# A decode step of attention plus a gated feed-forward layer: fewer and larger weight loads, and a new order of the last K and V

## The chip, the cores and the metric

The kernel runs on one core of a Trainium2 chip. The metric is the device time of one execution in microseconds (us). A profile gives a span some 2 us shorter than the device time of the same execution (523.8 us for 525.59 in the kernel before).

## The reference, cut to what matters

Four tokens (one for each of 4 sequences) are normalised, and the sum of three things is returned: x itself, sliding-window attention, and a gated feed-forward layer.

```python
xn = layernorm(x)                                    # (4, 1, 640)
q  = xn @ wq                                         # 32 heads of 192
s  = softmax(q . K[:, :, 6144:8192] / sqrt(192))     # the last 2048 of 8192 keys
y1 = (s . V[:, :, 6144:8192]).reshape(4, 1, 6144) @ wo                # wo (6144, 640)
y2 = (silu(xn @ w1) * (xn @ w3)) @ w2                # w1, w3 (640, 1536), w2 (1536, 640)
return x + y1 + y2
```

K and V of one head over the window and all four sequences are 3,072 KB each; 64 such loads are nearly all of the 223 MB that the kernel reads, and there is little arithmetic for each byte.

## The kernel before

All large loads are issued, in the order of the program, by one queue (the sync engine's, SPq in the profile). x's small load is issued by the scalar engine. The program is a table of slots, four for each head, and the sync engine waits for a buffer to be free before it issues the load into it. The parts that matter here:

```python
    def load_k(h):                                   # two K buffers
        kt = kpool.tile([P, NJ, Dh], BF16, tag="kt")
        nc.sync.dma_start(out=..., in_=k_win[:, h]...)
    def load_v(h, n=1):                              # three V buffers
        vt = vpool.tile([P, NJ, Dh], BF16, tag="vt")
    ...
    x_sb = const.tile([B, D], BF16, name="x_sb")
    nc.scalar.dma_start(out=x_sb[:], in_=A_x.rearrange("b s d -> (b s) d"))
    for k0 in range(0, KC, 2):                       # KC = 5: wq in three transfers, in V's buffers
        n = min(2, KC - k0)
        wt = vpool.tile([P, 2, H * Dh], BF16, tag="vt")
        nc.sync.dma_start(out=wt[:, 0:n, :]..., in_=wq_v[:, k0:k0 + n, :]...)
    for h in range(KBUFS):
        load_k(h)                                    # K0, K1
    # ... layer norm of x (vector and scalar engine), transposes of it (PE)
    # q = xn @ wq: two passes over six PSUM banks, 60 matmuls of 128x512, into qbc
    # ... clears of three PSUM tiles (vector engine)
    def mult(u):                                     # u = 4 h + g: quarter g of head h
        nc.vector.tensor_tensor(out=pr[:], in0=kts[h][:, g*JQ:(g+1)*JQ, :], in1=qbc[...], op=ALU.mult)
    ...
    for h in range(H):
        u0, ul = h * GQ, h * GQ + GQ - 1
        if h >= KBUFS:
            add((h - KBUFS + 1) * GQ, 0, load_k, h)  # K2 in slot 4: when K0's four products are done
        if h < H - 2:
            add(u0 + 2, 0, load_v, h)
        for u in range(u0, ul + 1):
            add(u, 1, mult, u)
    ...
    add(3, 0, w1_load)                               # 1.7 MB, between V0 and K2
    for n in range(4):
        add(4 + 2 * n, 1, w1_low, n)                 # w1's remaining rows, 12 partitions wide
    ...
    for h in range(H - 2, H):                        # the end of the queue
        add(NU - 6, 0, load_v, h)
    add(NU - 6, 0, w2_load, 0); add(NU - 6, 0, w2_load, 1)
    add(NU - 6, 0, wo_load, NG - 2); add(NU - 6, 0, wo_load, NG - 1)
    add(NU - 6, 0, w2_load, 2); add(NU - 6, 0, w2_load, 3)
```

So the first loads stand in the queue as wq, K0, K1 (issued at once), then V0 and w1 (when the projection has read wq's first two rows), then K2.

## Time and profile before

| | before |
|---|---|
| median of 3 runs | 525.7 us (525.61 to 526.16) |
| span of the profile | 523.8 us |
| busy: PE, vector engine (DVE), scalar engine (ACT) | 69%, 65%, 11% |
| load queue | 223.26 MB, 11,904 packets, 426 GB/s over the span |

The first view is the page's strip of 40 slices of 13.1 us: tenths in which the 16 load engines were busy, and what they moved.

```profile
DMA  9999999999999999999999999999999999999996
GB/s 389 422 443 425 433 431 432 428 433 432 430 435 428 437 418 446 424 437 426 434 434 429 432 434 429 435 427 435 425 437 434 427 437 431 430 434 425 441 418 275
```

Only the last slice is not full. Stretches of the span show the same (columns: length, busy time and instructions of PE, weight loads, DVE, ACT, POOL, then granted PE clock, share of the load engines' time, GB/s):

```profile
40.00:50.00 10.00, 6.59 (x31) 0.57 (x5) 8.79 (x9) 2.05 (x5) 0.00 (x0) 1.00 1.03 436
50.00:510.00 460.00, 325.19 (x2127) 69.40 (x1521) 311.62 (x358) 45.25 (x156) 0.00 (x0) 0.89 1.00 431
```

The load engines are busy from the first microseconds to the end (a share of 0.85 in the first 5 us, of 1.00 from 50 to 510), and no trace of this case moved more than 432 GB/s from 50 to 510 us. So the time of the kernel is the work in the queue, plus what stands before the first packet, plus what stands behind the last landing. The first part of the timeline of the sync queue, of DVE and of PE (start, length, engine, line, operation, count) shows how the head runs.

```profile
6.68 0.48 DVE L177 CAST xf<-x_sb 4x640 f32<-4x640 bf16 x1 [3.80 <-DMA x_sb<-in_A_x_dram]
```

PE, the projection:

```profile
15.15 14.93 PE L243 MATMUL qps<-wt,xnT 128*128 128x512 bf16 x59
```

And the sync queue, the issues of V0 and of K2:

```profile
26.22 0.54 SPq L132 DMA_DIRECT2D vt<-in_A_v_cache_dram  x1
...
41.62 0.54 SPq L125 DMA_DIRECT2D kt<-in_A_k_cache_dram  x1
```

The projection runs from 15.15 to about 30.1 us. The end, on PE:

```profile
519.21 0.98 PE L264 MATMUL acc<-wo_t,oT 128*4 128x320 bf16 x12 [0.47 <-DMA wo_t<-in_A_wo_dram]
520.38 0.71 PE L264 MATMUL acc<-w,hT 128*4 128x320 bf16 x8 [0.19 <-DMA w<-in_B_w_dram]
```

The same end in the chain of waits (start, length, what):

```profile
489.68 30.66 DMA w<-in_B_w_dram
520.38 0.76 PE acc L264 x8
521.13 0.47 DVE res L542
```

Three things were also read from the records of single packets in the trace, which have a start, a length, a size and a queue. Packets of one size take almost the same time everywhere: 9 ns for 4 B, 55 ns for 1,280 B, 912 ns for 24,576 B (the first ones of wq take 1.3 to 1.9 us, and 19 later ones, beside instruction fetches, 1.2 to 1.5); between the last two sizes that is 27.2 GB/s. The 16 engines do not end together: five end their last packet at 517.2 to 518.6 us, eleven at 519.6 to 520.5. And 15 packets of 16,384 B are instruction fetches and take about 0.94 us of an engine each. A "landing" below is the end of a load's last packet.

### The profile page before, as it was taken

The page shows a single profiled execution, that of the slowest core. Times are in us where ns is not written, and L with a number is a line of the kernel's source. Part 1 is how long each engine was busy: PE and PEld are TensorE (multiplying, and loading weights), DVE is VectorE, ACT ScalarE, POOL GpSimd, SP SyncE. Part 2 cuts the span into 40 slices and gives each one's busy share as a digit, 9 for nine tenths or more (in the row PEclk, how much of TensorE's full clock was granted, in tenths as well). Part 3 has the DMA queues.
Part 4 walks back from the last instruction along what each step waited for, and adds up shares of the span by engine and source line. Part 5 has one row for each costly group of instructions (what it writes and reads, how often), then busy time and mean ns, then how long its engine had stood idle before and what let it go on. Part 6 is the DMA issues. An engine that isn't in the chain of part 4 may idle for free.

```text
span 523.8 us, 4820 instructions
## 1 busy us (share of the span) xinstructions
PE 361.8 (69%) x2336; PEld 75.9 (14%) x1643; DVE 340.9 (65%) x413; ACT 55.8 (11%) x176; POOL 5.6 (1%) x12
## 2 busy tenths in 40 slices
PE   0965866887668776667547768586686876675685
PEld 0100111121111111111111111111111111111122
DVE  3268853687656767577646877466667766667671
ACT  2111111111001110101100111001101110011111
POOL 4000000000000000000000000000000000000000
PEclk9979886898878998789997988889878898889988
DMA  9999999999999999999999999999999999999996
GB/s 389 422 443 425 433 431 432 428 433 432 430 435 428 437 418 446 424 437 426 434 434 429 432 434 429 435 427 435 425 437 434 427 437 431 430 434 425 441 418 275
DMA packets 11904, 223.26 MB, mean 426 GB/s; under 512 B 1332, under 2 KB 1608, under 8 KB 3052
## 3 DMA queue, kind: packets, MB, share of 16 engines
q1 hardware_dynamic: 11868, 222.96, 99.2%
q8 instruction: 15, 0.25, 0.2%
q14 instruction: 5, 0.04, 0.0%
q10 hardware_dynamic: 16, 0.01, 0.0%
HBM read 222.96 MB, written 0.01 MB: 426 GB/s over the span
## 4 chain that ended last, share of the span: by engine, by line
DMA 60%; PE 20%; DVE 15%; ACT 3%; issue 1%; SPq 1%
DMA kt<-in_A_k_cache_dram 44%; PE ps L288 11%; DMA w<-in_B_w_dram 11%; DVE pr L277 10%; DMA vt<-in_A_v_cache_dram 5%; PE po L361 4%; PE qps L243 3%; DVE sc L296 2%; ACT ex L324 1%; DVE z L332 1%; DMA x_sb<-in_A_x_dram 1%; PE mt L318 1%; ACT L324 0%; ACT negm L321 0%; PE mt L305 0%
## 5 line engine op out<-in xcount | busy, mean ns | idle before, releaser
L288 PE MATMUL ps<-pr,idb 128*128 128x512 bf16 x768 | 214.7, 422 | 137.6 <-DVE pr L277 137.5
L277 DVE TENSOR_TENSOR pr<-kt,qbc 128x3072 bf16<-128x3072 bf16 x128 | 223.5, 1746 | 104.0 <-DMA kt<-in_A_k_cache_dram 104.0
L296 DVE TENSOR_REDUCE sc<-ps 128x16 f32<-128x512 f32 x128 | 87.1, 681 | 2.7 <-PE ps L288 2.6
L340 PE MATMUL o_ps<-vt,z 128*8 128x384 bf16 x1024 | 60.5, 380 | 0.2 <-DVE z L332 0.2
L361 PE MATMUL po<-o_sb,sel_w 128*32 128x192 f32 x128 | 49.2, 518 | 0.6 <-ACT o_sb L343 0.6
L340 PEld LDWEIGHTS <-z 128*8 128x8 bf16 x1024 | 26.2, 95 | 98.8 <-issue 89.2
L332 DVE TENSOR_TENSOR z<-ex,mask_b 128x256 bf16<-128x256 bf16 x32 | 13.5, 423 | 38.6 <-ACT ex L324 38.6
L343 ACT COPY o_sb<-o_ps 128x384 f32<-128x384 f32 x32 | 15.3, 478 | 196.9 <-PE o_ps L340 196.9
L313 ACT ACTIVATE gneg<-gmax 1x128 f32<-1x128 f32 x32 | 9.8, 308 | 162.8 <-DVE gmax L310 162.8
L305 PEld LDWEIGHTS mt<-idf,lmax 128*1 128x1 f32 x32 | 3.2, 101 | 127.5 <-issue 125.5
L361 PEld LDWEIGHTS po<-o_sb,sel_w 128*32 128x32 f32 x128 | 13.8, 130 | 29.4 <-issue 27.9
L288 PEld LDWEIGHTS <-idb 128*128 128x128 bf16 x124 | 12.0, 97 | 39.3 <-issue 32.8
L318 PEld LDWEIGHTS mt<-ones_ff,gneg 1*128 1x128 f32 x64 | 9.6, 186 | 47.1 <-issue 43.7
L243 PE MATMUL qps<-wt,xnT 128*128 128x512 bf16 x59 | 14.9, 412 | 0.1
L318 PE MATMUL mt<-ones_ff,gneg 1*128 1x1 f32 x64 | 12.3, 259 | 0.7 <-ACT gneg L313 0.7
L321 ACT COPY negm<-mt 128x1 f32<-128x1 f32 x32 | 5.1, 159 | 70.4 <-PE mt L318 70.4
L310 DVE TENSOR_REDUCE gmax<-mt 1x4 f32<-1x128 f32 x32 | 8.8, 274 | 5.8 <-PE mt L305 5.8
L348 PEld LDWEIGHTS po<-rsum,tot_w 128*32 128x32 f32 x64 | 4.4, 108 | 51.5 <-ACT ex L324 35.4
L249 DVE CAST qbc<-qps 128x512 bf16<-128x512 f32 x6 | 3.8, 684 | 11.7 <-PE qps L243 11.7
L324 ACT ACTIVATE ex<-sc,negm 128x64 bf16<-128x64 f32 x32 | 11.1, 348 | 1.0
L305 PE MATMUL mt<-idf,lmax 128*1 128x128 f32 x32 | 10.9, 340 | 0.0
L199 PE MATMUL xnT_ps<-idb,xn 4*128 4x4 bf16 x5 | 0.4, 178 | 13.4 <-DVE xn L194 13.4
(74 smaller groups left out, 84.4 us busy)
## 6 DMA issues: line engine op xcount, KB each, us to landing
kt<-in_A_k_cache_dram SPq DMA_DIRECT2D x32, 3072.0 KB, 19.1
vt<-in_A_v_cache_dram SPq DMA_DIRECT2D x32, 3072.0 KB, 25.5
wo_t<-in_A_wo_dram SPq DMA_DIRECT2D x8, 960.0 KB, 20.7
wt<-in_A_wq_dram SPq DMA_DIRECT2D x2, 3072.0 KB
w<-in_B_w_dram SPq DMA_DIRECT2D x1, 1920.0 KB
wt<-in_A_wq_dram SPq DMA_DIRECT2D x1, 1536.0 KB, 19.5
w<-in_B_w_dram SPq DMA_DIRECT2D x1, 1536.0 KB
w<-in_B_w_dram SPq DMA_DIRECT2D x2, 640.0 KB
```

Source lines behind the costliest of these rows:

```text
L243: nc.tensor.matmul(qp[:], lhsT=xnT[:, kc].rearrange("p a b -> p (a b)"), rhs=wq_rows[kc][:, (c0 + i) * QC:(c0 + i + 1) * QC], start=(kc == ...
L277: nc.vector.tensor_tensor(out=pr[:], in0=kts[h][:, g * JQ:(g + 1) * JQ, :], in1=qbc[:, h * Dh:(h + 1) * Dh].unsqueeze(1).to_broadcast([P, ...
L288: nc.tensor.matmul(ps[:], lhsT=idb[:], rhs=pr[:, :, kk * DD:(kk + 1) * DD], start=(kk == 0), stop=(kk == NK - 1))
L296: nc.vector.tensor_reduce(out=scs[h][:, g * JQ:(g + 1) * JQ], in_=pss.pop(u)[:], axis=AX.X, op=ALU.add)
L305: nc.tensor.transpose(out=mt[0:1, 0:P], in_=chs[h][0][:], identity=idf[:])
L313: nc.scalar.activation(out=gneg[:], in_=gmax[:].unsqueeze(1).to_broadcast([1, PB, B]), func=ACTF.Copy, scale=-SCALE)
L318: nc.tensor.matmul(mt[:, P:P + 1], lhsT=gneg[:].rearrange("o p b -> o (p b)"), rhs=ones_ff[:], start=True, stop=True)
L324: nc.scalar.activation(out=ex[:], in_=scs.pop(h)[:], func=ACTF.Exp, bias=negm[:, 0:1], scale=SCALE, accum_out=rsum[:])
L332: nc.vector.tensor_tensor(out=z[:], in0=ex[:].unsqueeze(2).to_broadcast([P, NJ, B]), in1=mask_b[:].unsqueeze(1).to_broadcast([P, NJ, B]), ...
L340: nc.tensor.matmul(o_ps[c * CT:c * CT + 2 * B, :], lhsT=z[:, 2 * jj:2 * jj + 2, :], rhs=vt[:, 2 * jj:2 * jj + 2, :], start=(jj < 4), stop= ...
L343: nc.scalar.copy(out=o_sb[:], in_=o_ps[:])
L361: nc.tensor.matmul(po[sl, 0:Dh], lhsT=sel_w[:, par].rearrange("p a b -> p (a b)"), rhs=o_sb[:, par * Dh:(par + 1) * Dh].rearrange("p (r i) ...
```

## The change

The intent is to pay less for packets and transfers in a queue that is always full, and to shorten the end: wo in four groups of eight heads instead of eight groups of four, wq in two transfers instead of three, w2 in one instead of four, w1's remaining 72 rows in two transfers instead of 64 rows in four, the last K ahead of the last three V so that the last softmax is done before the last V lands, and wo's last group behind everything in three pieces. The three V buffers become one tile, in which wq's larger pieces fit. The core of the diff (cuts marked):

```diff
-    HG: int = 4,
+    HG: int = 8,
+    FG: int = 4,
...
+    v_all = vpool.tile([P, VBUFS * NJ * Dh], BF16, name="v_all")
...
     def load_k(h):
-        kt = kpool.tile([P, NJ, Dh], BF16, tag="kt")
+        kt = k_buffer() if h < H - 1 else v_buffer()
...
-    def load_v(h, n=1):
+    def load_v(h):
+        vt = v_buffer() if h < H - 1 else k_buffer()
...
-    for k0 in range(0, KC, 2):
-        n = min(2, KC - k0)
-        wt = vpool.tile([P, 2, H * Dh], BF16, tag="vt")
-        nc.sync.dma_start(out=wt[:, 0:n, :].rearrange("p k n -> p (k n)"),
-                          in_=wq_v[:, k0:k0 + n, :].rearrange("p k n -> p (k n)"))
+    wq_t = v_all[:, 0:KC * H * Dh].rearrange("p (k n) -> p k n", k=KC)
+    for k0, k1 in ((0, 3), (3, KC)):
+        nc.sync.dma_start(out=wq_t[:, k0:k1, :].rearrange("p k n -> p (k n)"),
+                          in_=wq_v[:, k0:k1, :].rearrange("p k n -> p (k n)"))
...
+        nc.sync.dma_start(out=ffn["w1e"][n * CT:n * CT + LP].rearrange("p s n -> p (s n)"),
+                          in_=B_w1[b0:b0 + LS * LP, :].rearrange("(i e s) n -> e i (s n)", e=LE, s=LS))
...
-    ends = {H - 2: (NU - 1, NU), H - 1: (NU + 3, NU + 4)}
+    ends = {H - 3: (NU - 1, NU), H - 2: (NU + 2, NU + 3), H - 1: (NU + 4, NU + 5)}
+    early = {H - 1: (NU - 10, -1)}
     for h in range(H):
         if h >= KBUFS:
-            add((h - KBUFS + 1) * GQ, 0, load_k, h)
+            add(*early.get(h, ((h - KBUFS + 1) * GQ, 0)), load_k, h)
...
-    for n in range(4):
-        add(4 + 2 * n, 1, w1_low, n)
+    for n in range(2):
+        add(5 + 3 * n, 1, w1_low, n)
...
+    WOC = [0, RPP - 5, RPP - 2, RPP]
     for h in range(H - 2, H):
         add(NU - 6, 0, load_v, h)
-    add(NU - 6, 0, w2_load, 0)
-    ... (w2 in four pieces around wo's last two groups)
+    add(NU - 6, 0, w2_load)
+    for i0, i1 in zip(WOC, WOC[1:]):
+        add(NU - 6, 0, wo_load, NG - 1, i0, i1)
+        add(e, 6, ge_proj, NG - 1, i0, i1, True)
+    add(e - 1, 8, ffn_out)
```

## The prediction

> **What bounds the kernel now.** The load queue. The 40-slice strip shows DMA at 9 in every slice but the last; a table of stretches gives a DMA share of 1.00 and 429 to 433 GB/s from 14 to 510 us. PE (69% busy) and DVE (65%) follow: DVE's largest wait is for K tiles (104.0 us). [...] The chain of waits ends in the last w2 load (landed 520.38), 0.76 us of 8 matmuls, a 0.47 us copy and the store.
>
> **(a) Less work in the queue.** Packet times in the trace are almost constant: 1,280 B takes 55 ns, 7,680 B 291, 24,576 B 912, and successors start 3 to 4 ns before a packet's end. So a packet costs about 5 ns beyond its bytes at 27.2 GB/s; a transfer's semaphore packet about 10 ns on each engine. The change saves per engine 8 packets of wq, 16 of wo, 24 of w2: 48 x 5 = 0.24 us, and 6 transfers over all 16 engines, 0.06 us: about -0.3 us. w1's half rows keep their size (64 rows loaded, 8 of them with zero weights).
>
> **(b) Balance of its engines.** w1's remaining rows go in transfers whose outer size is 3. [...] 24 packets of 6,144 B run three at a time. They carry about 197 KB before, 221 KB after (72 rows, not 64): +0.30 us on those three, which I read as among the last to finish (ends of the engines' last data: five at 517.2 to 518.6, eleven at 519.6 to 520.5 us). There (a) is about cancelled; the last landing moves by -0.3 to +0.1 us.
>
> **(c) Tail.** Behind the last V still come 3.93 MB (w2, one wo group), 9.1 us, as before. Last K now lands some 22 us before the last V, so the last head's softmax leaves the tail (before: pv at 513.3 to 516.0). After: V lands near 511.4, pv 1.5 to 2.7 us, copy 0.5, sums 1.5, og about 0.6, transpose about 0.65 (twice as wide as 0.42 and 0.38): oT near 517, ahead of wo's first piece (~518.6). Behind the last landing stay 4 matmuls instead of 8: -0.35 us.
>
> **(d) Head.** The first wq piece lands near 12 us, before the first matmul (14.5); the other when the old third did. PE may wait 0.5 us; the queue then holds work to about 33 us and V0's issue (26.2) has slack. Nothing.
>
> HG=8 halves DVE's group work (0.96 us a group): off the critical path.
>
> **Sum.** 525.7 - 0.15 (queue) - 0.35 (tail) = **525.2 us**, range 524.4 to 526.0. Faster by over 2%: 0.01; within 2%: 0.97; slower by over 2%: 0.02.
>
> **What would show it.** DMA share 1.00 up to about 518 us; packets fall from 11,904 to about 11,000; last weight landing within 0.3 us of 520.4; the chain's end shows wo, then 4 matmuls (about 0.4 us), then the copy; DVE's waits for K unchanged.
>
> **What would make it wrong.** A false wait between V loads now that they share one tile, which would empty the queue (share below 1.00 mid-span); wo's single buffer or the K/V ring swap stalling an issue near the end; a halved PE clock making the last projection lag its loads (the tail's gain goes).

## The result, and the profile after

The changed kernel takes 527.81 us (median of 6 runs, 527.08 to 528.21) against 525.72 (6 runs, 525.61 to 526.16) in the same rounds: ratio 1.0036, 95% interval 1.0023 to 1.0049. It is the same within 2%, as predicted, but it is clearly slower, by 2.1 us, where 0.5 us less was predicted, and it lies outside the range of 524.4 to 526.0.

The page of the profile after has fewer packets (11,010 for 11,904) at slightly lower overall rate. The strip shows where:

```profile
DMA  9999999999999999999999999999999999999995
GB/s 387 430 435 389 428 433 428 432 441 425 434 431 432 434 431 432 429 433 432 431 434 430 434 433 430 432 433 432 432 432 430 437 426 435 429 434 431 432 429 231
```

The fourth slice (39.5 to 52.6 us) has 389 GB/s; it had 425 before. The digit is still 9: a tenth that is only partly lost is easily missed in the strip. The stretches confirm it:

```profile
40.00:50.00 10.00, 7.50 (x30) 0.19 (x3) 9.76 (x11) 0.31 (x1) 0.00 (x0) 0.90 0.96 391
50.00:510.00 460.00, 321.58 (x2128) 69.11 (x1517) 312.25 (x350) 47.46 (x161) 0.00 (x0) 0.89 1.00 432
```

From 50 to 510 us the queue is as good as before (432 GB/s). Between 40 and 50 it moves 391 GB/s, not 436: (436 - 391) x 10 us is 0.45 MB, about 1 us of the whole queue. The head runs later throughout. DVE of the changed kernel:

```profile
7.91 0.48 DVE L191 CAST xf<-x_sb 4x640 f32<-4x640 bf16 x1 [5.02 <-DMA x_sb<-in_A_x_dram]
```

PE, the projection:

```profile
16.11 15.99 PE L259 MATMUL qps<-v_all,xnT 128*128 128x512 bf16 x59
```

The sync queue, V0 and K2:

```profile
28.25 0.53 SPq L147 DMA_DIRECT2D v_all<-in_A_v_cache_dram  x1
...
43.80 0.54 SPq L141 DMA_DIRECT2D kt<-in_A_k_cache_dram  x1
```

DVE sees x 1.23 us later, the projection lasts 1.06 us longer, and K2 is issued at 43.80, 2.18 us later. The end on PE:

```profile
520.89 1.74 PE L280 MATMUL acc<-wo_t,oT 128*4 128x320 bf16 x20 [0.87 <-DMA wo_t<-in_A_wo_dram]
522.85 0.44 PE L280 MATMUL acc<-wo_t,oT 128*4 128x320 bf16 x4 [0.21 <-DMA wo_t<-in_A_wo_dram]
```

The end of the chain of waits:

```profile
488.15 34.66 DMA wo_t<-in_A_wo_dram
```

In the packets the last weights land at 522.52 us, 2.0 us later than the 520.48 of before; the matmuls that wait for them start at 522.85 here and at 520.79 before (of the 8 in the line that begins at 520.38, only the last two; see (c) below). The chain still ends in a load.

The records of the packets tell more of the 40 to 50 us stretch. In the changed kernel the engines run out of packets from 45.9 us on: five of the sixteen get their first packet of K2 0.8 to 1.6 us after their last packet of w1, others at once, and near 49 us many wait again in the middle of K2, or take 1.3 to 1.6 us for a packet that usually takes 0.91. I count as lost the time in which an engine has no packet, plus what a packet takes over its usual time, summed over the 16 engines: **16.4 us of engine time between 40 and 50 us in the changed kernel, 0.6 before** (0.53 of that beside one instruction fetch). From 50 to 60 us the changed kernel loses some 2 us more. In 10 to 40 us and from 60 us on both have next to none but what the instruction fetches cost.

16.4 over 16 engines is 1.0 us, but the last engine ends 2.0 us later (522.52 for 520.48), and the ends now spread from 517.8 to 522.5. The loss is unequal, each engine carries about the same share (526 to 529 of the 8,448 packets of 24,576 B before, in the chains of packets described next), and a transfer has landed only when the last engine is done. The records do not name the engines, so one engine's loss was not followed to its end; but packets of an engine can be chained, because each starts as another ends (within 4 ns in the trace of before), and the sixteen last ends read without names. Their mean is 520.35 us in this trace, and 519.27 and 519.29 in two later traces of the changed kernel that lost nothing (after2 and a_clear, below): 1.1 us, which is the loss of 40 to 60 us over 16 engines. The last engine ends 2.2 us behind this mean here and 1.4 behind it there. So one half of the 2 us is the loss itself and the other a wider spread; where the loss was even over the engines (b_late2, below), the mean moved by 1.20 us against the kernel before and the last end by 1.25. That the unequal loss makes the spread is likely from this, but not followed engine by engine.

**Why is the head late?** Two parts, both visible in the packets and in PE's record.

1. x's four small packets (1,280 B, on the scalar engine's queue) run behind three or four packets of wq: they start at 4.80 to 5.35 us before, behind packets of 24,576 B (0.91 us each, the first ones 1.3 to 1.9), and at 5.69 to 6.13 after, behind three packets of 36,864 B (1.36 us each, the first ones 1.4 to 2.4). In all traces where x's load was not edited, DVE sees x at 6.68 to 7.00 us with wq in three transfers and at 7.91 to 8.31 with wq in two, so this part belongs to the change. The layer norm, the transposes and the projection all wait for x.
2. The first 8 matmuls of the projection start 0.43 us apart before (called slow below), the later ones 0.22; in the changed kernel the first 13 are slow. 5 x 0.21 us is the 1.06 us by which it is longer. The traces of these kernels with no edit to PE have 7 to 14 slow ones (7 and 13 in two traces of the changed kernel itself). The packed traces also record when the clock was granted in full: the first such record is at 18.43 us before, 21.56 in this trace and 19.25 in after2, just where the slow matmuls end. So the second part is not of the change; it varies from trace to trace.

### The profile page after: what moved, and what is told of

The parts are those of the page before. It is cut to its first block, busy times and chain, and to the rows that moved or that the text cites. A ratio compares the mean times of both kernels' runs of the same rounds, so it can differ in the third digit from the quotient of the medians. Undisturbed runs are those within 1.5% of the kernel's fastest.

```text
span 526.0 us, 4773 instructions
## 1 busy us (share of the span) xinstructions
PE 359.5 (68%) x2327; PEld 75.2 (14%) x1633; DVE 339.6 (65%) x398; ACT 55.9 (11%) x176; POOL 5.5 (1%) x11
## 2 busy tenths in 40 slices
DMA packets 11010, 223.28 MB, mean 424 GB/s; under 512 B 1230, under 2 KB 1366, under 8 KB 1622
## 4 chain that ended last, share of the span: by engine, by line
DMA 60%; PE 21%; DVE 16%; ACT 3%; issue 1%; SPq 0%
DMA kt<-in_A_k_cache_dram 52%; PE ps L305 11%; DVE pr L294 11%; DMA wo_t<-in_A_wo_dram 7%; PE po L378 4%; PE qps L259 3%; DVE sc L313 2%; DMA x_sb<-in_A_x_dram 1%; ACT ex L341 1%; DVE z L349 1%; PE mt L335 1%; PE acc L280 1%; ACT L341 0%; ACT negm L338 0%; PE mt L322 0%
## 5 line engine op out<-in xcount | busy, mean ns | idle before, releaser
L294 DVE TENSOR_TENSOR pr<-kt,qbc 128x3072 bf16<-128x3072 bf16 x124 | 216.5, 1747 | 103.8 <-DMA kt<-in_A_k_cache_dram 103.8
L357 PE MATMUL o_ps<-v_all,z 128*8 128x384 bf16 x992 | 54.5, 364 | 0.4 <-DMA v_all<-in_A_v_cache_dram 0.4
L349 DVE TENSOR_TENSOR z<-ex,mask_b 128x256 bf16<-128x256 bf16 x32 | 13.6, 424 | 34.5 <-ACT ex L341 34.4
L259 PE MATMUL qps<-v_all,xnT 128*128 128x512 bf16 x59 | 15.9, 433 | 0.1
L280 PE MATMUL acc<-wo_t,oT 128*4 128x320 bf16 x96 | 9.6, 308 | 1.1 <-DMA wo_t<-in_A_wo_dram 1.1
```

The lines of the kernel that those rows point to most:

```text
L259: nc.tensor.matmul(qp[:], lhsT=xnT[:, kc].rearrange("p a b -> p (a b)"), rhs=wq_rows[kc][:, (c0 + i) * QC:(c0 + i + 1) * QC], start=(kc == ...
L280: nc.tensor.matmul(acc[i * CT:i * CT + B, :], lhsT=lhsT, rhs=rhs[:, i * N0:(i + 1) * N0], start=first, stop=last)
L294: nc.vector.tensor_tensor(out=pr[:], in0=kts[h][:, g * JQ:(g + 1) * JQ, :], in1=qbc[:, h * Dh:(h + 1) * Dh].unsqueeze(1).to_broadcast([P, ...
L349: nc.vector.tensor_tensor(out=z[:], in0=ex[:].unsqueeze(2).to_broadcast([P, NJ, B]), in1=mask_b[:].unsqueeze(1).to_broadcast([P, NJ, B]), ...
L357: nc.tensor.matmul(o_ps[c * CT:c * CT + 2 * B, :], lhsT=z[:, 2 * jj:2 * jj + 2, :], rhs=vt[:, 2 * jj:2 * jj + 2, :], start=(jj < 4), stop= ...
```

## The experiments

Theory A: the late head makes K2's issue late, the queue runs dry at 45.9 us, and the engine time lost there is the whole result. Rivals: B, the wider rows of w1 on three load engines, or the new order of K and V, set the engines apart; C, the two large wq transfers do harm in some other way than by K2; D, the late head is carried to the end by PE and DVE. All variants gave correct results. In each diff `+` and `-` are against the kernel named. The names starting with a_ are variants of the changed kernel, those with b_ of the kernel before.

**a_wq3** (changed kernel):

```diff
-    for k0, k1 in ((0, 3), (3, KC)):
+    for k0, k1 in ((0, 2), (2, 4), (4, KC)):
```

> The changed kernel with wq back in three transfers (rows 2, 2, 1: packets of 24,576 B). Theory (the two wq transfers, with 36,864 B packets, hold x's small load back; the head runs late, K2 is issued too late and the load queue runs dry at 46 to 50 us): x's load is seen by the vector engine near 6.7 us as before (7.9 in the changed kernel), the projection ends 1 to 2 us earlier, no hole at 46 to 50 us, and the time is 525.0 to 525.6, about 2.3 us under the changed kernel. Rival (w1's 72 low rows on three load engines, or the swap of the last K and V, make the engines end apart): still 527.3 to 528.

Measured: 525.83 us (525.53 to 526.14; before 526.01 in the same rounds, with single runs up to 527.52), ratio 0.9993 (0.9981 to 1.0005). DVE saw x at 6.87 us, K2 was issued at 42.58, 2.0 us of engine time were lost, the last landing was at 520.52. B falls: w1's rows and the K and V order are still the changed ones. The projection still had 12 slow matmuls and ended only 1.2 us earlier, and the median is 0.2 us over the expected range.

**a_x_head** (changed kernel; a pass over the finished program moves x's load on the scalar queue to the place where the first wq transfer already stands):

```diff
+        act = mybir.EngineType.Activation
+        i, ins = next((i, ins) for i, ins in enumerate(body.instructions)
+                      if ins.engine == act and isinstance(ins, mybir.InstDMACopy))
+        del body.instructions[i]
+        head.instructions.insert(j, ins)     # j: before the scalar engine's drain in the head block
```

> The changed kernel with x's load issued by the scalar queue at the program's head, beside the first wq transfer, not 0.8 us later. Theory: x then lands before wq's packets pile up, 2 to 4 us earlier than now; the whole head moves ahead by at least 1 us (limited by wq's first landing near 14 us), the hole at 46 to 50 us goes, time 524.8 to 525.6, although wq stays in two transfers. If instead the second wq landing (near 21 us) is what holds the projection, or the rival of the unequal load engines holds, the time stays above 527.

Measured: 525.68 us (525.58 to 526.02), ratio 0.9993 (0.998 to 1.0006). x's packets ran at 2.96 to 4.00 us, K2 was issued at 41.40, 0.6 us was lost, last landing 520.37. wq is in two transfers here, so their size does no harm once x is early. (The median is 0.1 us over the expected range, far from the rival's 527.)

**a_v1_early** (changed kernel):

```diff
-            add(u0 + 2, 0, load_v, h)
+            add(3 if h == 1 else u0 + 2, 0, load_v, h)
```

> The changed kernel with V1's load issued ahead of w1 and K2, so that the queue holds 7.3 us more work while K2 waits for its buffer. The head stays as late as in the changed kernel. Theory (the head's lateness costs only through the empty queue): K2 is still issued near 43.8 us, no hole at 46 to 50, time 524.9 to 525.7. Rival (the late head itself is carried to the end by PE and DVE): no gain, 527.3 to 528.

Measured: 527.03 us (526.26 to 528.05), ratio 1.002 (1.0006 to 1.0033): missed. Nothing was lost at 40 to 50 us; but K2 was issued at 42.04 in this trace, early enough to lose nothing in any case (see the table below), so it does not test whether the fuller queue closes the hole. And 13.8 us of engine time were lost at 70 to 80: K2 now stood behind V1, 3 MB more, so its products and with them the issue of K4 (73.75 us, for 65.31 before) came too late. The stretch in which that load was missing:

```profile
70.00:80.00 10.00, 8.11 (x57) 1.74 (x42) 7.72 (x9) 1.08 (x4) 0.00 (x0) 0.83 0.98 399
```

The new order opened a hole of its own. Here the last projection also fell behind its loads: PE's clock was recorded at half from 517.8 to 521.2 us, the matmuls found wo landed without a wait, and the last pair started at 522.21, 0.6 us behind the last landing (521.62). This is the third thing that the prediction had listed as able to make it wrong; it was not seen in the first trace of the changed kernel.

**b_wq2** (kernel before): only wq in two transfers, with V's three buffers in one tile.

```diff
-    for k0 in range(0, KC, 2):
-        ...wt = vpool.tile([P, 2, H * Dh], BF16, tag="vt")...
+    for k0, k1 in ((0, 3), (3, KC)):
+        ...wq_t = v_all[:, 0:KC * H * Dh]...
```

> The kernel before with only wq in two transfers (3 and 2 rows, V's three buffers in one tile for it). Theory: this part alone makes x late by about 1.2 us, K2's issue later by 1 to 2 us and a hole in the queue near 46 us: 526.5 to 528, that is 1 to 2.3 us slower than before. Rival (the cause lies in another part of the change): 525.4 to 526.

Measured: 526.16 us (525.72 to 526.67; before 526.01), ratio 1.0 (0.9988 to 1.0012): missed. x was late (8.22), the projection ended late and K2 was issued at 43.69, all as theory A says, but only 0.9 us of engine time was lost: every engine got its first packet of K2 just in time. So lateness of this size is on the edge, and it does not always cost.

**after2** (the changed kernel, unedited, once more):

> The changed kernel again, unedited, for a second trace. If the hole in the load queue is the cause, it is there again near 46 to 50 us, the last landing is near 522 and the time 527 to 528.2. If a hole is absent while the time is still 527 or more, the hole is not the cause.

Measured: 526.58 us (525.96 to 527.61, 4 runs; before 525.71), ratio 1.0019 (1.0005 to 1.0034). The expectation that the hole is always there missed, and the miss is worth more than a hit. The run that was profiled took 525.96 us: 7 slow matmuls in the projection where the first trace had 13, K2 issued at 41.86, nothing lost at 40 to 50, last landing 520.69. Its stretch of 40 to 50 us, and then K2's issue in its sync queue:

```profile
40.00:50.00 10.00, 6.60 (x31) 0.57 (x5) 9.04 (x10) 1.81 (x4) 0.00 (x0) 1.00 1.00 428
```

The sync queue of after2:

```profile
41.86 0.54 SPq L141 DMA_DIRECT2D kt<-in_A_k_cache_dram  x1
```

The same program differs by 2 us between two runs, and K2's issue and the loss go with it. The two traces are from different sessions: all six runs of the first lay at 527.08 to 528.21, the four of this one at 525.96 to 527.61. So the lateness is not drawn afresh in each run alone; what else the sessions differed in (the chip, for one) was not tested, and the cost of the change is anything from 0.9 to 2.1 us by the two medians.

**b_late2** (kernel before): five dummy operations on DVE behind x's arrival.

```diff
+    late = const.tile([P, 512], FP32, name="late")
+    for _ in range(5):
+        nc.vector.tensor_scalar_add(out=late[0:B, :], in0=xf[:, 0:512], scalar1=1.0)
     ssum = const.tile([B, 1], FP32, name="ssum")
```

> The kernel before, with five small dummy operations on the vector engine between x's load and its statistics: the head later by some 2.2 us, K2 issued near 43.8 us as in the changed kernel, and nothing else changed. Theory (a late K2 alone empties the queue): a hole near 46 us and 526.5 to 528. The run with only wq in two transfers had K2 at 43.69 and no hole, which speaks for the rival: lateness of this size costs little by itself (525.6 to 526.4), and something else in the changed kernel makes K2's packets start late.

Measured: 526.7 us (525.8 to 527.07; before 525.71), ratio 1.0012 (1.0 to 1.0024): as the theory expected, though the interval only just clears 1. K2 was issued at 45.13, later than aimed at (16.22 us of projection, with 14 slow matmuls), 19.3 us of engine time were lost, quite evenly over the engines, and the last landing was at 521.73. The stretch:

```profile
40.00:50.00 10.00, 6.36 (x28) 0.18 (x2) 9.48 (x10) 0.00 (x0) 0.00 (x0) 0.98 0.93 377
```

K2's issue in the sync queue of b_late2:

```profile
45.13 0.55 SPq L125 DMA_DIRECT2D kt<-in_A_k_cache_dram  x1
```

The kernel before, with nothing but a later head, loses in the same place.

**a_wq3_late1** (changed kernel with a_wq3's edit and three of the same dummy operations):

> The changed kernel with wq in three transfers and three dummy vector operations: K2 issued near 43.9 us, as in the changed kernel, but wq's packets small. Theory of the late K2 issue: the hole is back and the time is 526.8 to 528. Rival (the two big wq transfers do the harm in another way than by lateness): no hole, 525.5 to 526.2.

Measured: 527.36 us (525.62 to 527.48; six runs in two groups, four at 527.3 to 527.5 and two at 525.6 to 525.8), ratio 1.0018 (1.0004 to 1.0031). In the profiled run (527.34) K2 was issued at 43.15 and 11.0 us were lost, with small wq packets, as the theory expected: C falls. The two groups show the edge once more: the head either makes it or does not.

**a_low_later** (changed kernel):

```diff
-        add(5 + 3 * n, 1, w1_low, n)
+        add(7 + 2 * n, 1, w1_low, n)
```

> The changed kernel with w1's two low-row transfers (12 rows of 9,216 B, on three load engines) issued after V1 and V2, not between K2 and V1. If this small transfer, wider than before, slows the supply of K2's packets, the hole at 46 to 50 us goes and the time falls to 525.5 to 526.2. If it has no part in it (my expectation), the hole stays and the time is 527 to 528.2.

Measured: 527.24 us (525.91 to 528.21; before 525.71), ratio 1.0023 (1.001 to 1.0037). K2 issued at 43.50, 4.3 us lost, most of it on three or four engines (single packets 0.8 to 1.2 us over their time), last landing 521.92. The small transfer is not the cause, as expected. Less was lost than in the first trace of the changed kernel, with nearly as late an end.

**a_warm** (changed kernel): 40 dummy matmuls of zeros ahead of the transposes.

```diff
+    busy = const.tile([P, QC], BF16, name="busy")
+    nc.vector.memset(busy[:], 0.0)
+    warm = ps_add.tile([P, QC], FP32, tag="ps", name="warm")
+    for n in range(40):
+        nc.tensor.matmul(warm[:], lhsT=idb[:], rhs=busy[:], start=True, stop=True)
```

> The changed kernel with 40 dummy matmuls (128x512, zeros) ahead of the first transposes; wq stays in two transfers and x stays late (near 8 us). Theory (half of the lateness is the projection's first 8 to 14 matmuls at 0.43 us each where later ones take 0.22; their number is chance): the projection's matmuls start at 0.22 us, it ends near 29 us, K2 is issued near 41 us, no time is lost in the queue at 40 to 50 us, 525.4 to 526.0 and little spread from run to run. Rival (it is x's lateness alone that counts, or the hole has another cause): 526.5 to 528.

Measured: 526.01 us (525.82 to 526.72; before 525.84), ratio 0.9998 (0.9984 to 1.0012). The time came about as expected and the reason did not: the dummies ended at 13.6 us, and the projection, from 16.47, still had 8 slow matmuls in the profiled run (526.72), K2 at 43.15, 4.5 us lost. It cannot be told from this whether the clock helped in the other runs. Inconclusive.

**a_head** and **b_head**: the head mended in both. a_head is the changed kernel with the edits of a_wq3, a_x_head and a_warm and with `WOC = [0, RPP - 5, RPP - 1, RPP]`; b_head is the kernel before with those of a_x_head and a_warm.

> The changed kernel with the whole head mended: wq in three transfers, x's load at the head, 40 dummy matmuls, and wo's last piece one row (2 matmuls behind the last landing, not 4). Theory: K2 issued before 41 us, no loss at 40 to 50, last landing 520.2 to 520.5, time 525.2 to 525.6: what the change's own savings are worth with the loss gone, 0.1 to 0.5 us under before. Rival (the other parts of the change cost something too): 526 or more.

> The kernel before with x's load at the head and 40 dummy matmuls. It had no loss at 40 to 50 us in its trace, so the theory expects no gain in its usual runs, 525.4 to 525.8; only its slower single runs (526 to 527.5, seen in two sessions), if they come from the same late head, should vanish. Rival (an earlier head is worth something by itself): under 525.2.

Measured: a_head 525.84 us (525.56 to 526.25), ratio 0.9994 (0.998 to 1.0008); b_head 525.88 (525.66 to 526.52), 0.9996 (0.9982 to 1.0011); before 525.84 with single runs up to 527.7. K2 at 41.41 and 41.57, 1.1 us lost in each, last landing 520.42 and 520.45. The 40 dummies held PE to about 15 us, which spent what the earlier x had gained. No saving of the change is seen, so the expectation for a_head (525.2 to 525.6) missed. b_head's two slower runs (526.18 and 526.52) have spans of 523.8 and 524.1 us like the others, so what made them slower lies outside the profiled span and says nothing of K2.

**a_head_w8** (a_head, with w1's last 128 rows in one transfer of outer size 8, to move load to engines that end early):

```diff
-        nc.sync.dma_start(out=wt[:, FM:], in_=...)                 # half rows, all engines
-        nc.sync.dma_start(out=ffn["w1e"][n * CT:n * CT + LP]...)   # 72 low rows, three engines
+        nc.sync.dma_start(out=ffn["w1e"][:].rearrange("p s n -> p (s n)"),
+                          in_=B_w1[KM * P:D, :].rearrange("(i e s) n -> e i (s n)", e=8, s=2))
```

> The mended changed kernel with w1's last 128 rows all in one transfer whose outer size is 8 (64 rows of 6,144 B), in place of the half rows over all engines and the 72 low rows on three. [...] the last landing moves from 520.3 to about 519.9 and the time to 524.8 to 525.2. [...] 525.8 to 526.8.

Measured: 528.43 us (528.15 to 529.53), ratio 1.0047 (1.0033 to 1.0061): missed on both ranges. Both are the author's estimates and rest on which engines carry the instruction fetches and which the transfer; the records do not name the engines, so neither case was shown. While the transfer ran, packets of 24,576 B were slow as well (up to 1.62 us), not only its own. The stretch in a_head_w8:

```profile
50.00:58.00 8.00, 4.15 (x38) 1.04 (x33) 4.70 (x6) 0.48 (x1) 0.00 (x0) 0.79 1.01 353
```

The same stretch in the kernel before:

```profile
50.00:58.00 8.00, 5.57 (x46) 1.04 (x36) 6.36 (x8) 0.62 (x3) 0.00 (x0) 0.79 1.01 432
```

The rate (last column) is 353 for 432 GB/s. Packets of 24,576 B took up to 1.62 us, the transfer's own 64 packets up to 0.77 us for a usual 0.23, and 23.8 us of engine time were lost at 50 to 60. The three-engine transfers of both kernels run at full pace (0.23 us for 6,144 B, 0.35 for 9,216). What the packets collide with is open.

**a_clear** (changed kernel; wq and x untouched): the clears of three PSUM tiles moved behind K0's fourth product.

```diff
-        nc.vector.memset(o_ps[:], 0.0)     # two, before K0's first product
...
-    nc.vector.memset(acc[:], 0.0)
...
+    add(3, 9, clear)                       # the same three, in slot 3, behind the product
```

> The changed kernel with three clears of PSUM (1.1 us on the vector engine) moved from before K0's first product to after its fourth: K2's buffer is free about 1.1 us sooner; wq and x are as in the changed kernel, x still late. Theory (only the time of K2's issue counts): K2 issued between 40.8 and 42.7 us, less than 3 engine-us lost at 40 to 50 us, median 525.7 to 526.5. Rival (wq's two large transfers or x's lateness do the harm by some other way than K2): 526.8 to 528 with K2 issued before 42.5.

Measured: 525.88 us (525.64 to 526.01; before 525.77), ratio 0.9998 (0.9985 to 1.0012). Its stretch of 40 to 50 us:

```profile
40.00:50.00 10.00, 5.97 (x27) 0.57 (x5) 9.84 (x13) 0.52 (x3) 0.00 (x0) 1.00 1.00 428
```

DVE, when x arrives:

```profile
8.31 0.48 DVE L191 CAST xf<-x_sb 4x640 f32<-4x640 bf16 x1 [5.43 <-DMA x_sb<-in_A_x_dram]
```

The sync queue, K2:

```profile
41.98 0.54 SPq L141 DMA_DIRECT2D kt<-in_A_k_cache_dram  x1
```

x was as late as ever (8.31 us), wq in two transfers, and K2's issue at 41.98 was enough: 0.0 us lost, last landing 520.64. This is the cleanest test: D falls, since the head was late up to the clears and nothing of it was carried to the end, and C falls again.

**a_clear_x** (a_clear with the edits of a_wq3 and a_x_head) and **b_clear_x** (the kernel before with the clears moved and a_x_head's edit):

> The changed kernel with the clears moved, wq in three transfers and x's load at the head: K2 issued near 40 us, nothing lost, no run over 526.3; median 525.4 to 525.9. It shows what the rest of the change is worth beside the kernel before with the same head (next run): theory, equal within 0.3 us, since the queue's saving does not reach the engines that end last and the tail gains nothing.

> The kernel before with the clears moved and x's load at the head: K2 issued near 39.5 us, nothing lost, median 525.5 to 525.9, as the kernel before in its usual runs, and no slower single runs (526.2 and more), if those come from a late K2.

Measured: a_clear_x 525.74 us (525.64 to 525.88), ratio 0.9997 (0.9984 to 1.001); b_clear_x 525.54 (525.47 to 525.8), 0.9994 (0.9982 to 1.0007); before 525.77 (525.65 to 526.81). K2 issued at 37.81 and 38.55, 0.6 us lost in each, last landing 520.34 and 520.31. b_clear_x has the lowest median of all kernels tried, but its gain over the kernel before is not clear of noise; that it has no slow single run in five fits a head with room to spare, and five runs do not prove it.

The traces together, in the order of K2's issue (lost: engine time at 40 to 50 us, worked out from the packets, in the four rows with 0.6 nearly all of it beside an instruction fetch; the time is that of the profiled run). a_head and b_head, with 1.1 lost beside two fetches, and the two runs that lost elsewhere are left out:

| trace | K2 issued, us | lost, us | last landing, us | profiled run, us |
|---|---|---|---|---|
| a_clear_x | 37.81 | 0.6 | 520.34 | 525.77 |
| b_clear_x | 38.55 | 0.6 | 520.31 | 525.50 |
| a_x_head | 41.40 | 0.6 | 520.37 | 525.67 |
| before | 41.62 | 0.6 | 520.48 | 525.59 |
| after2 | 41.86 | 0.0 | 520.69 | 525.96 |
| a_clear | 41.98 | 0.0 | 520.64 | 525.92 |
| a_wq3 | 42.58 | 2.0 | 520.52 | 525.90 |
| a_wq3_late1 | 43.15 | 11.0 | 521.92 | 527.34 |
| a_warm | 43.15 | 4.5 | 521.44 | 526.72 |
| a_low_later | 43.50 | 4.3 | 521.92 | 527.24 |
| b_wq2 | 43.69 | 0.9 | 520.94 | 526.16 |
| after (first trace) | 43.80 | 16.4 | 522.52 | 527.83 |
| b_late2 | 45.13 | 19.3 | 521.73 | 526.87 |

With K2 issued by 42 us nothing is lost but beside fetches. From 42.6 on K2's packets reach some engines too late, how late differs from trace to trace, and the end does not follow the sum alone: with 4.3 us lost (a_low_later) the mean of the sixteen ends is only 0.3 us over after2's, but the last end is 1.2 over. That it follows the engines that lost most is likely, not followed through.

## Why the prediction was wrong, point by point

**The step that failed is (d), the head**: "The first wq piece lands near 12 us, before the first matmul (14.5); the other when the old third did. PE may wait 0.5 us; the queue then holds work to about 33 us and V0's issue (26.2) has slack. Nothing." Three things are wrong in it.

- The head's clock is x's load, not wq's landing. Larger wq packets ahead of it made x 1.23 us later in the first trace of the changed kernel. The wait of 0.5 us on wq that was feared did not occur: the 13 first matmuls follow each other at an even 0.43 us.
- The wrong load was tested for slack. V0 did have slack. The next one, K2, is issued only when DVE has done K0, and the queue behind V0 and w1 ends at about 46 us. K2's issue at 41.62 in the kernel before left 4.3 us until then, and the runs show that some 3.5 us are needed: with 42.58 the loss begins (an estimate from the table; b_wq2, at 43.69, lost almost nothing). The slack was about one microsecond, and it was never worked out.
- The number of slow first matmuls was taken from one trace as if it were fixed. It ranged from 7 to 14 in traces with no edit to PE, which is 1.5 us of chance in an interval that had one microsecond to spare. The single trace of before showed a usual or lucky case (single runs of the kernel before reach 526.8 to 527.7 us in the later sessions), and the later x of the changed kernel leaves nothing to spare for it.

**(a) The queue's work was right.** -0.3 us per engine was predicted. In the clean pair, the packets of the main queue add up to 519.59 us per engine in a_clear_x and 519.91 in b_clear_x: -0.32 us.

**(b) Balance was right in its direction**, and no gain reached the last landing, which was predicted to move by -0.3 to +0.1 us and moved by +0.03 in the pair (520.34 for 520.31). The -0.15 us booked for it in the sum was too good by as much. That the three engines with w1's low rows are among the last, and eat up the gain, was read, not tested.

**(c) The tail was wrong in its size, by its sign.** "Behind the last landing stay 4 matmuls instead of 8: -0.35 us." The last V did land with its softmax done, and the last projection waited only for its loads (gaps of 0.87 and 0.21 us behind wo in the lines after), as predicted. But the 8 matmuls at 520.38 in the timeline before are two groups in one line: the first 6 belong to the piece of w2 that had landed before, and only the last two, which start at 520.79, stand behind the last landing (520.48 in the packets). The change put 4 there for 2. From the last landing to the end of the span it is 3.39 us in b_clear_x (523.7 - 520.31) and 3.66 in a_clear_x (524.0 - 520.34): +0.27 us where -0.35 was booked. Over all traces whose tail was not edited it is 3.32 to 3.39 us in the five of the kernel before and 3.46 to 3.66 in nine of the changed one (a_v1_early, where PE fell behind, left out): +0.18 us between the means, never a gain. a_head, with one row in the last piece, had 3.58 (524.0 - 520.42), no clear gain: the piece ahead of it then lands late as well, and 10 matmuls of 0.84 us stand at the end.

**The sum.** With the loss gone, the changed kernel is 0.2 us over the kernel before with the same head (525.74 and 525.54), not 0.5 under: +0.03 for the landing and +0.27 for the tail, which fits. The runs of the two overlap (525.64 to 525.88 and 525.47 to 525.80), so the 0.2 is not clear of noise; that a saving of 0.5 is absent is, by the spread of these ten runs. The remaining 2 us of the result are the loss at 40 to 50 us and the wider spread of the ends that comes with it.

**What "would make it wrong" had listed** (a false wait between V loads, a stall near the end, a halved clock in the tail) named an empty queue as the sign, and that was the right sign. It looked for it in the middle and at the end, not at the head, where buffers are released for the first time.

**Open**: why K2's packets come to some engines only 3.8 us after the issue and to others within 1.9 (43.80 to 47.56 and to 45.74 in the first trace after), why b_wq2 lost little with K2 as late as 43.69, why packets in the middle of K2 wait again near 49 us, what sets the first session apart from after2's, and whether work on PE just ahead of the projection keeps its first matmuls from being slow (the projection took 13.32 us in a_head and b_head, where the dummies ended at about 15 us, and had 8 slow matmuls in a_warm, where they ended at 13.6).

## What to carry to other kernels

When the load queue is the bound, work out for each load of the head how long the queue still has work when it is issued, and hold that against the time that its packets need to arrive; the thinnest such margin decides, and a load that waits for the compute of an earlier one is the likely place. A tiny load that starts the whole chain should be issued ahead of the large ones, because here it waited for three or four packets of the load issued before it, one when it was issued beside that load (a_x_head, 2.96 to 4.00 us), and for longer when these packets were larger (5.69 to 6.13 us behind 36,864 B, 4.80 to 5.35 behind 24,576 B). Take a second trace of a changed kernel before explaining the first: two runs of the same program differed by 2 us here, and the difference was the explanation.

## What else the traces show

- The first packet of wq, with all engines idle, started 1.0 us after its issue began (0.00 to 1.00 in the trace of before). With the queue running dry after 45 us of full load, the engines that stood empty got their first packets of K2 2.8 to 3.8 us after its issue began (43.80 to 46.59 and to 47.56 in the first trace after).
- On one core, 431 to 432 GB/s were moved for 460 us (50 to 510 us, before and after).
- With one transfer of outer size 8 in the queue, 353 GB/s were moved from 50 to 58 us in a_head_w8, for 432 before (the cause is open).
- The number of slow matmuls (0.43 us apart, not 0.22) is not to be counted on: 7 and 13 in two traces of one program. 5 slow matmuls more, 1.06 us, helped to empty the queue.
- A trap of the views: they give a clock of 1.00 for 15 to 20 us in the trace of before, while the matmuls start 0.43 us apart, because the trace has no clock record before 18.43 us. In a_warm, where there is one, the views read 0.50 for 16.7 to 20.1 us, where its 8 slow matmuls stand.
